# Requesting expert weights and K/V rows in two halves on one DMA queue

## The chip, the cores and the metric

The kernel runs on one core of a Trainium2 chip. The core has five engines that run side by side: TensorE (PE; its weight loads are PEld), VectorE (DVE), ScalarE (ACT), GpSimd (POOL) and SyncE (SP), which here only issues DMA requests. All DMA requests of SyncE go into one queue that 16 DMA engines work off. The metric is the device time of one execution in microseconds; the median of several runs is compared.

## The reference, cut to what matters

Attention with a pooled K/V, and behind it a mixture of experts that sends every row to one expert:

```python
# attention: q (4, 12288, 128), kv (4, 384, 32, 128)
kv_pool = kv.reshape(B, H // 4, 4, W // 4, 4, C).mean(axis=(2, 4))
k = v = kv_pool.reshape(B, -1, C) @ w_sr          # 768 rows of 128 for each b
a = softmax(q @ k.T / sqrt(C)); x = a @ v
# experts: 49152 rows of 128, E = 8 experts, F = 1024
expert_idx = argmax((x / |x|) @ (emb / |emb|).T / tau)
for e in range(E):
    h = np.maximum(x[mask] @ w1[e], 0.0)
    out[mask] = gate_w[mask, None] * (h @ w2[e])
```

## The kernel before

**Attention.** The 49152 rows of q are worked off in 96 steps of 512 (`step_ops`). A step has four score tiles of 128 x 768 (`s_mm`, L810), each evicted by VectorE (`s_leave`, L821) and put through an exponential on ScalarE (L840). Products are made of 16-bit high and low parts: the probabilities are split into `phi` (L861, L865) and `plo` (L875, L880), both are turned by DMA transposes on SyncE into `pthi` and `ptlo` (`p_t`, L904), two score tiles at a time, and `av` (L926) multiplies 12 times with pthi and 6 times with ptlo for each tile. From step 21 on q is turned by DMA as well (`q_turn`, L790).

**K/V.** For b = 1 to 3 the rows of K/V come in eight loads each (`kv_load`, L453): 96 partitions, 4 rows (r) of 2048 bytes, 768 KB. Two buffers `kvt` take turns. Four adds (`kv_adds`, L467) fold a load into `pooled`; the first adds rows 2 and 3 to rows 0 and 1. They run on VectorE for b = 1 and 3 and on GpSimd for b = 2, and stand in those engines' order with everything else.

**Routing.** Each group of four steps is ranked by expert (L1008 to L1151), its rows are scattered to `xs_rows` in HBM (L207), and `select` then picks the next eight tiles of 256 rows, one expert a tile.

**Experts.** Weights are split once at the start into 16-bit parts and stored to `w_prep` in HBM (`w_hi`, `w_lo`, `w_store`). A row of a partition holds first-layer high and low (2 x 1024 elements), second-layer high and low (2 x 1024), and then a scale (8 elements, 4 copies of one 32-bit number): 8208 bytes. For tile t, `load_w` (L1568) copies the 128 rows of its expert, 1026 KB, into one of three buffers `wbuf`; the copy is conditional, and is skipped where that buffer already holds the expert. `load` (L1592, L1593) brings the tile's rows, turned, and their gates. A tile has 8 units of 512: `l1` (L1625) multiplies with the first layer, ScalarE and VectorE evict into `hh` (L1632) and `hl` (L1637), `l2` and `l2_lo` (L1661) multiply with the second layer some units later, into `po`. The scale is needed by VectorE: in `o_gate` (L1672), which multiplies the gates with it while the tile is still running, or, for two tiles of eight (`X["om"]`), in `o_out` (L1684) at its end. There are 184 tiles of 256 rows (`NA`) and up to 23 of 128; requests for tiles under `NA - PER` = 176 are made one by one, the rest in fours.

**Order.** Nothing is reordered on the chip: each engine runs its instructions in the order in which they are written, and a request that waits on SyncE holds those behind it. The order comes from a planner (`Plan`): every operation has an engine, a modelled duration, a key and the operations that it waits for; the planner plays the engines forward and takes, on each, the ready operation with the least key. For a DMA it also models the transfer (`dma`, in us) and holds SyncE back while earlier transfers run:

```python
self.moved = max(self.moved, op.end + 0.65) + op.dma
if eng == "SP":
    turned = op.dur > 0.5
    free[eng] = max(free[eng] + (0.55 if turned else 0.0), self.moved - (0.93 if turned else X["ahead"]))
```

`X["ahead"]` is 2.284. A K/V load has a duration of 0.45 and a transfer of 2.6, a turn of p 0.63 and 1.8, a tile's load 2.5 and 0.65; a copy of weights has 0.5 and a transfer of 3.6 for the first three tiles and 0.08 after them, since most copies are skipped. Keys of l2 lie `X["l2"]` = 3.102 units behind those of l1, a unit being an eighth of 14.892.

Of the kernel before, what the change touches and what calls it, by code (L numbers as in the profile page):

```python
# [11 lines left out]
F16 = mybir.dt.float16  # L12
F32 = mybir.dt.float32
# [4 lines left out]
ALU = mybir.AluOpType  # L18
# [12 lines left out]
ENG = {"A": "ACT", "D": "DVE", "P": "POOL"}  # L31
# [7 lines left out]
KV_ADD = {"D": (1.13, 0.6, 0.33, 0.2), "P": (2.4, 1.25, 0.7, 0.45)}  # L39
# [9 lines left out]
    h=13.707, kv=20.916, kvs=2.272, w0=-14.405, start=23.312, early=21.36, wd=12.952, xw=1.718, qd=21, qs=21.178,  # L49
    ql=9.747, em="---------AA-A-A-A-AA-DM-", et=2.859, ec=-0.864, v0=123.118, sd=1, qu=1.461, q0=-66.525, avd=0.626,  # L50
    m=1.052, end=-3.563, ne=-4.766, ge=-0.689, kd="DPD", gk=547.052, wq="AADADDAD", kv1=10.617, kvs1=0.757, tg=-0.003,
# [8 lines left out]
def attention_moe(  # L60
# [11 lines left out]
    nc = tc.nc  # L72
    V = nc.vector
    P = 128
    B, N, C = q.shape
    H, W = kv.shape[1], kv.shape[2]
    E, _, F = w1.shape
    NT = B * N
    R = 4
    NI, NJ = H // R, W // R  # L80
# [13 lines left out]
    PER = G * Q // T  # L94
    NSEL = NGRP - LAG
    NA = NSEL * PER
# [7 lines left out]
    XB = 6  # L104
    PTB = 4
    PB = 3
    Q2 = 3
    NP = 6
    QB = 2
    NQR = 8  # L110
    WC = 4 * F + 8
    WD = 4 * F + 32
    SCALE = 1.0 / math.sqrt(C)
    PSC = 16384.0
    QSC = 16384.0
# [2 lines left out]
    KF = X["kf"]  # L118

    xs = nc.dram_tensor("xs_rows", (NROW, RP), F32).ap()  # L120
    wprep = nc.dram_tensor("w_prep", (E * P, WD), F16).ap()[:, :WC]
    qf = q.rearrange("b n c -> (b n) c")

    cpool = ctx.enter_context(tc.tile_pool(name="cpool", bufs=1))
# [12 lines left out]
        out=window.rearrange("p (g q) -> p g q", q=4), in_=ident.rearrange("p (g m q) -> p g q m", m=4, q=4), axis=AX.X,  # L137
        op=ALU.add,
# [5 lines left out]
        out=tri16, in_=ones16, pattern=[[1, P]], compare_op=ALU.is_gt, fill=0.0, base=0, channel_multiplier=-1  # L144
# [55 lines left out]
    nt_i = cpool.tile([P, 1], I32, name="nt_i")  # L200
    off_i = cpool.tile([P, NTILE], I32, name="off_i")
    wi_i = cpool.tile([P, NTILE], I32, name="wi_i")
    cpool.tile([P, 72], F32, name="fill")
    ctx.enter_context(tc.manual_schedule())

    def scatter(dst, idx, src, bound, key, skip=()):
# [47 lines left out]
    class Plan:  # L254
# [9 lines left out]
        def add(self, eng, dur, key, fn, *deps, dma=None, take=None, free=None, hold=False, lands=False, port=False):  # L264
            op = Op(eng, dur, key, fn, deps, dma, take, free, hold, lands, port, self.stage)
            self.ops.append(op)
            return op
# [23 lines left out]
        def run(self, begin):  # L291
# [23 lines left out]
            while any(count):  # L315
# [7 lines left out]
                for eng in soon:  # L323
                    if now.setdefault(eng, []):
                        t = free.get(eng, 0.0)
# [77 lines left out]
                            free[eng] + (0.55 if turned else 0.0), self.moved - (0.93 if turned else X["ahead"])  # L403
                        )
                for u in op.users:
                    if op.dma is not None and u.dma is not None and eng == u.eng and not op.lands:
                        ready = op.end
                    elif op.dma is not None:
                        ready = self.moved + X["dma"]
                    else:  # L410
                        ready = op.end + lat.get((eng, u.eng), 0.0)
                    u.ready = max(u.ready, ready)
                    u.left -= 1
                    if not u.left:
                        put(u)
# [33 lines left out]
    def kv_load(b, h):  # L449

        t = kvs.tile([P, WD // 2], F32, tag="kvt", name=f"kvt{b}_{h}", bufs=2)
        t = t[:NI, : R * QC].rearrange("p (r c) -> p r c", r=R)
        nc.sync.dma_start(  # L453
            out=t, in_=kv[b].rearrange("(i r) w c -> i r (w c)", r=R)[:, :, h * QC : (h + 1) * QC]
        )
        st[b]["kvt", h] = t

    def kv_pooled(b, h):
        if h == 0:
# [739 lines left out]

    def w_out(e, i):  # L1200

        wo = xp.tile([P, 2 * F + 8 * i], F16, tag=f"wo{i}", name=f"wo{e}_{i}", bufs=1)
        ws[e]["wo", i] = wo
        if i:
            inv = ws[e]["inv"]
            V.tensor_tensor(
                out=wo[:, 2 * F :].bitcast(F32), in0=inv[:, 0:1].broadcast_to([P, 4]),
                in1=inv[:, 1:2].broadcast_to([P, 4]), op=ALU.mult,
            )

    def w_mul(e, i):
# [6 lines left out]
    def w_hi(e, i):  # L1218
        if i == 0:
            w_out(e, 0)  # L1220
        hi = ws[e]["wo", i][:, 0:F]
        if w_eng(e, i) == " AD":
            nc.scalar.mul(hi, ws[e]["w", i], ws[e]["s"][:, i : i + 1])
        else:
            nc.scalar.copy(out=hi, in_=ws[e]["w", i])

    def w_lo(e, i):
        hi, lo = (ws[e]["wo", i][:, h * F : (h + 1) * F] for h in range(2))
        if w_eng(e, i) == " AD":
            V.scalar_tensor_tensor(  # L1230
                out=lo, in0=ws[e]["w", i], scalar=ws[e]["s"][:, i : i + 1], in1=hi, op0=ALU.mult, op1=ALU.subtract
            )
        else:
            nc.gpsimd.tensor_tensor(out=lo, in0=ws[e]["w", i], in1=hi, op=ALU.subtract)
# [2 lines left out]
        return W_MODES[X["we"][2 * e + i]]  # L1237

    def w_store(e, i):
        nc.sync.dma_start(out=wprep[e * P : (e + 1) * P, 2 * i * F : WC if i else 2 * F], in_=ws[e]["wo", i])  # L1240


    def setup(key, *deps):
# [319 lines left out]
    def load_w(t):  # L1563
        if NA <= t < NA + 2:
            wbuf.append(kvs.tile([P, WD], F16, tag="kvt", name=f"wbuf{WB + t - NA}", bufs=2))
        w = value("w", wi_i, t, E * P + 4096)
        row = nc.s_assert_within(w, 0, (E - 1) * P, skip_runtime_bounds_check_because="the copy is skipped then")
        nc.sync.dma_start(out=wbuf[turn_of(t)][:, :WC], in_=wprep[ds(row, P), :], cond=w < E * P)  # L1568

    xr, late = [], []  # L1570
    ML = 18
# [29 lines left out]
    def turn_of(t):  # L1601
        return t % WB if t < NA else (WB, WB + 1, *[(NA + i) % WB for i in range(WB)])[(t - NA) % (WB + 2)]

    def weights(t, a, n):
        return wbuf[turn_of(t)][:, a : a + n]
# [48 lines left out]
    def l2_terms(t, u, h, parts):  # L1654

        n = size(t)
        fu, nj = 512 // n, n // P
        terms = [(kk, j, o) for kk in range(fu) for j in range(nj) for o in parts]
        for i, (kk, j, o) in enumerate(terms):
            f = 2 * F + (u * fu + kk) * P + o  # L1660
            nc.tensor.matmul(  # L1661
                ts[t]["po"][:, j * C : (j + 1) * C], h[:, kk * n + j * P : kk * n + (j + 1) * P], weights(t, f, P),
                start=u == 0 and i == 0 and len(parts) == 2,
                stop=u == units(t) - 1 and i == len(terms) - 1 and len(parts) == 1, skip_group_check=True,
            )
# [3 lines left out]

    def o_gate(t):  # L1670
        m = ts[t]["m"][:, :, 0:1]
        V.tensor_scalar(out=m, in0=m, scalar1=weights(t, 4 * F, 2).bitcast(F32), scalar2=None, op0=ALU.mult)  # L1672

    def o_out(t):
        m = ts[t]["m"]
        nj = size(t) // P
        if gated(t):
            o = ts[t]["o"] = wk2.tile([P, nj, C], F32, tag="o", name=f"o{t}", bufs=OB)
            po = ts[t].pop("po").rearrange("p (j c) -> p j c", c=C)
            for j in range(nj):  # L1680
                nc.scalar.mul(o[:, j, :], po[:, j, :], m[:, j, 0:1])  # L1681
            return
        o = wk2.tile([P, nj, C], F32, tag="o", name=f"o{t}", bufs=OB)
        V.scalar_tensor_tensor(  # L1684
            out=o, in0=ts[t].pop("po").rearrange("p (j c) -> p j c", c=C),
            scalar=weights(t, 4 * F, 2).bitcast(F32), in1=m[:, :, 0:1].broadcast_to([P, nj, C]),
            op0=ALU.mult, op1=ALU.mult,
        )
        ts[t]["o"] = o
# [19 lines left out]
    def turn(tag, bufs):  # L1709

        u = uses.setdefault(tag, [])
        return (u[-1][:1] if u else []) + (u[-bufs] if len(u) >= bufs else [])

    def took(tag, op):
        uses[tag].append([op])
        return op

    def reads(tag, *ops):
        uses[tag][-1].extend(ops)

    x_wsr = add("ACT", 0.1, -60.0, lambda: nc.scalar.dma_start(out=wsr[:, 0:C], in_=w_sr), dma=0.2)
    x_tau = add("ACT", 0.1, -60.0, lambda: nc.scalar.dma_start(out=tau_b, in_=tau.broadcast_to([P, 1])), dma=0.06)
    x_emb = add("ACT", 0.1, -60.0, lambda: nc.scalar.dma_start(out=emb_sb, in_=emb), dma=0.02)
# [24 lines left out]
    def kv_ops(b):  # L1748
        mine = [None] * NQR
        for h in range(NQR if b else 0):  # L1750
            ahead, apart = (X["kv1"], X["kvs1"]) if b == 1 else (X["kv"], X["kvs"])
            t0 = slot(b * SPB, -8 * (ahead - h * apart))
            o = took("kvt", add("SP", 0.45, t0, lambda h=h: kv_load(b, h), *turn("kvt", 2), dma=2.6, hold=True))
            deps = turn("pooled", 1) if h == 0 else mine[h - 1 : h]
            r = None
            on = X["kd"][b - 1]
            for i, fn in enumerate(kv_adds(b, h, V if on == "D" else nc.gpsimd)):
                r = add(ENG[on], KV_ADD[on][i], t0 + 8.0 + 0.1 * i, fn, o, r, *deps, port=True)
                reads("kvt", r)
            if h == 0:  # L1760
                took("pooled", r)
            mine[h] = r
# [397 lines left out]
    for t in range(NTILE):  # L2160
# [14 lines left out]
            "SP", 0.5 if t < NA - PER else 0.2 if t % 4 else 1.2, kw, lambda t=t: load_w(t), *deps[:2], *stores, *wb_turn(t),  # L2175
            dma=3.6 if t < WB or first or NA + 1 < t < NA + 7 else 0.08, hold=first,
        ))
        o1, o2, ol = None if whole else o1, None, None
        f = 512 / size(t)
        for u in range(nu):  # L2180
            key = s + (u + X["m"]) * w
# [76 lines left out]
```

## Time and profile before

| | us |
|---|---|
| median of 3 runs (lowest, highest) | 1948.01 (1947.91, 1948.92) |
| profiled execution | 1946.91 |
| its span, first to last instruction | 1945.2 |
| busy: TensorE / weight loads | 1906.0 / 1676.3 |
| busy: VectorE / ScalarE / GpSimd | 1675.1 / 1468.7 / 1289.4 |

The span is what the trace covers; 1.7 us of the execution lie around it. An engine's busy time is a union over its instructions. SyncE computes nothing: its rows are requests, each from the moment it is taken up to the moment it is issued, so that a row that is long for its kind waited for something, data or room. Windows give the busy time of each engine in a stretch, the granted TensorE clock (1.00 is 2.4 GHz, 0.50 is 1.2 GHz) and the busy share of the 16 DMA engines, which counts a packet's whole time where it starts and so can pass 1.

### The profile page before, as it was taken

What the parts mean: (1) busy time and instruction counts of PE and PEld (TensorE: products, weight loads), DVE (VectorE), ACT (ScalarE), POOL (GpSimd) and SP (SyncE); (2) the same over time, 40 slices, a digit from 0 to 9 for tenths busy, and PEclk for the clock granted to TensorE, in tenths of its full rate; (3) what the DMA queues carried; (4) which work ended last, traced back from release to release, by engine and by line L of the source; (5) the groups of instructions that cost most, each with busy time, mean ns of one, the idle gap of its engine ahead of it and who ended that gap; (6) DMA issues with size and microseconds to landing.
All of it is one profiled execution on the core that took longest, in us unless ns stands there. A gap on an engine that the chain in (4) does not pass through costs nothing. (4 is left out here: it accounts for less than half of the span.)

```text
span 1945.2 us, 63642 instructions
## 1 busy us (share of the span) xinstructions
PE 1906.0 (98%) x23536; PEld 1676.3 (86%) x23536; DVE 1675.1 (86%) x4037; ACT 1468.7 (76%) x3162; POOL 1289.4 (66%) x1857
## 2 busy tenths in 40 slices
PE   6999999999999999999999999999999999999998
PEld 5787788888888888888888888888888888889998
DVE  7899999988989879989989988998888888886655
ACT  4887877877787778877778877878878788775553
POOL 2547587678777777676676675756756766666654
PEclk9999999999999999999999999999999999999999
DMA  7998989889988999878989899887878677664353
GB/s 258 250 267 207 205 174 183 165 156 164 170 182 173 190 205 175 172 165 157 193 168 175 180 214 180 171 157 155 176 132 173 149 153 152 148 126 86 107 131 109
DMA packets 870922, 333.23 MB, mean 171 GB/s; under 512 B 825794, under 2 KB 836171, under 8 KB 868432
## 3 DMA queue, kind: packets, MB, share of 16 engines
q1 hardware_dynamic: 844624, 274.95, 71.4%
q0 software_dynamic: 24640, 53.53, 9.7%
q8 instruction: 186, 3.05, 0.7%
q14 instruction: 128, 1.05, 0.2%
q10 hardware_dynamic: 1344, 0.66, 0.1%
HBM read 271.41 MB, written 63.19 MB: 172 GB/s over the span
## 5 line engine op out<-in xcount | busy, mean ns | idle before, releaser
L1632 ACT ACTIVATE hh<-ph 128x512 f16<-128x512 f32 x754 | 447.6, 595 | 224.4 <-PE ph L1625 181.2
L1637 DVE SCALAR_TENSOR_TENSOR hl<-ph,hh 128x512 f16<-128x512 f32 x754 | 513.6, 684 | 109.6 <-ACT hh L1632 103.7
L1625 PE MATMUL ph<-x,wbuf 128*128 128x256 f16 x4416 | 593.2, 273 | 3.2 <-DMA wbuf<-w_prep 2.5
L207 POOL DMA_INDIRECT xs_rows<-rows,pi x384 | 442.0, 1151 | 176.5 <-issue 37.8
L207 POOL DMA_INDIRECT out_dram<-o,m x350 | 382.4, 1093 | 229.0 <-ACT o L1681 45.8
L1625 PEld LDWEIGHTS <-wbuf 128*128 128x128 f16 x4848 | 438.9, 98 | 67.4 <-DMA wbuf<-w_prep 2.9
L1661 PE MATMUL po<-wbuf,hh 128*128 128x128 f16 x6032 | 459.9, 219 | 2.9 <-DVE hl L1637 1.1
L1661 PEld LDWEIGHTS <-hh 128*128 128x128 f16 x6176 | 400.0, 98 | 20.6 <-issue 3.8
L810 PE MATMUL s<-k,qT 128*128 128x512 f16 (+1 forms) x1920 | 364.9, 326 | 1.4 <-DVE nm L821 1.4
L821 DVE CUSTOM_DVE_ANT_0 p<-s,scales,qa 128x768 f32<-128x768 f32 x320 | 323.4, 1011 | 41.6 <-PE s L810 38.9
L875 DVE SCALAR_TENSOR_TENSOR plo<-p,phi 128x768 f16<-128x768 f32 x358 | 350.3, 980 | 5.6 <-ACT phi L861 2.4
L840 ACT ACTIVATE p<-p,nm 128x768 f32<-128x768 f32 x320 | 299.0, 934 | 58.8 <-DVE nm L821 56.8
L926 PE MATMUL xp<-v,pthi 128*128 128x136 f16 (+1 forms) x4392 | 319.7, 223 | 1.4 <-ACT q L738 0.8
L1661 PE MATMUL po<-wbuf,hl 128*128 128x128 f16 x3016 | 291.6, 219 | 0.0
L926 PEld LDWEIGHTS <-pthi 128*128 128x128 f16 x4392 | 278.7, 98 | 14.4 <-issue 2.3
L861 ACT ACTIVATE phi<-p 128x768 f16<-128x768 f32 x310 | 260.9, 844 | 5.9 <-DMA pthi<-phi 2.8
L810 PEld LDWEIGHTS <-qT 128*128 128x128 f16 x1920 | 178.6, 98 | 87.4 <-issue 2.3
L1661 PEld LDWEIGHTS <-hl 128*128 128x128 f16 x3088 | 205.1, 98 | 0.6
L926 PE MATMUL xp<-v,ptlo 128*128 128x136 f16 x2196 | 189.8, 223 | 4.3 <-DMA ptlo<-plo 4.3
L946 ACT ACTIVATE x<-xp,rn 128x135 f32<-128x135 f32 x304 | 96.5, 372 | 76.3 <-DVE rn L938 58.2
L960 POOL TENSOR_TENSOR rows<-x,rows 128x256 f16<-128x256 f32 x192 | 137.2, 719 | 18.2 <-ACT rows L956 13.3
L926 PEld LDWEIGHTS <-ptlo 128*128 128x128 f16 x2196 | 144.0, 98 | 4.8 <-DMA ptlo<-plo 4.8
(416 smaller groups left out, 2043.0 us busy)
## 6 DMA issues: line engine op xcount, KB each, us to landing
wbuf<-w_prep SPq DMA_DIRECT2D x202, 1026.0 KB
q<-in_q_dram SPq DMA_DIRECT2D x48, 512.0 KB
kvt<-in_kv_dram SPq DMA_DIRECT2D x24, 768.0 KB
wf<-in_moe_w_dram SPq DMA_DIRECT2D x16, 512.0 KB
kvt<-in_kv_dram SPq DMA_DIRECT2D x12, 512.0 KB
xs_rows<-rows,pi POOLq DMA_INDIRECT x384
out_dram<-o,m POOLq DMA_INDIRECT x350
w_prep<-wo SPq DMA_DIRECT2D x8, 514.0 KB
```

The lines of the kernel that those rows point to most:

```text
L207: ins = nc.gpsimd.indirect_dma_start(out=dst, out_offset=bass.IndirectOffsetOnAxis(ap=idx, axis=0), in_=src, in_offset=None, bounds_check= ...
L810: nc.tensor.matmul(t[:, lo:hi], qs[:, l, :], r[:, lo:hi], start=i == 0, stop=i == 2)
L821: V.tensor_tensor_reduce(out=p, in0=ks[k].pop(("s", j)), in1=scales[:, 4:5].broadcast_to([P, NK]), scale=ks[k]["fac"], scalar=3.0e38, op0= ...
L840: nc.scalar.activation(out=p, in_=s, func=AF.Exp, bias=ks[k].pop(("nm", j)), scale=1.0 if unscaled(k) else -1.0)
L861: nc.scalar.mul(hi, p, PSC)
L875: V.scalar_tensor_tensor(out=lo, in0=ks[k].pop(("p", j)), scalar=PSC, in1=hi, op0=ALU.mult, op1=ALU.subtract)
L926: nc.tensor.matmul(ks[k]["xp", h][:, i, :e], l[:, c, :], r[:, c, :e], start=n == 0, stop=n == len(terms) - 1, skip_group_check=True,)
L960: nc.gpsimd.tensor_tensor(out=r[:, :, C : 2 * C], in0=ks[k]["x"][:, 2 * h : 2 * h + 2, 0:C], in1=r[:, :, 0:C], op=ALU.subtract)
L1625: nc.tensor.matmul(ph[:, kk * n : (kk + 1) * n], weights(t, o + f, P), r, start=i == 0, stop=i == 2)
L1632: nc.scalar.activation(out=hh, in_=ts[t]["ph", u], func=AF.Relu)
L1637: V.scalar_tensor_tensor(out=hl, in0=ts[t].pop(("ph", u)), scalar=0.0, in1=ts[t]["hh", u], op0=ALU.max, op1=ALU.subtract)
L1661: nc.tensor.matmul(ts[t]["po"][:, j * C : (j + 1) * C], h[:, kk * n + j * P : kk * n + (j + 1) * P], weights(t, f, P), start=u == 0 and i ...
```

## The change

A row of `w_prep` becomes 8256 bytes: the scale moves from the end to the place between the two layers and is 32 elements wide. For tiles under 176 the copy is requested in two halves, first layer and scale, then second layer; the second half has the same condition. l1 and the scaling of the gates read the first half, l2 the second. Loads of K/V are requested in two halves of two rows (r) each; the first add waits for both. `second` makes the request of the second half: an operation of no duration on SyncE whose key is lower than all others, behind an operation on an engine `"~t"` that stands for nothing on the chip and takes 1.5 us (`HALF`) from the modelled end of the first request. Whole copies remain for tiles from 176 on.

```diff
+    HALF = 1.5
-    WC = 4 * F + 8
-    WD = 4 * F + 32
+    WS = 32
+    WD = 4 * F + WS
...
-                    if op.dma is not None and u.dma is not None and eng == u.eng and not op.lands:
+                    if op.dma is not None and u.dma is not None and eng == u.eng and not op.lands or u.eng == "~t":
                         ready = op.end
...
     def kv_load(b, h):
...
+        kv_part(b, h, 0)
+
+    def kv_part(b, h, i):
+        r = slice(i * (R // 2), (i + 1) * (R // 2))
         nc.sync.dma_start(
-            out=t, in_=kv[b].rearrange("(i r) w c -> i r (w c)", r=R)[:, :, h * QC : (h + 1) * QC]
-        )
+            out=st[b]["kvt", h][:, r, :],
+            in_=kv[b].rearrange("(i r) w c -> i r (w c)", r=R)[:, r, h * QC : (h + 1) * QC],
+        )
...
-                out=wo[:, 2 * F :].bitcast(F32), in0=inv[:, 0:1].broadcast_to([P, 4]),
-                in1=inv[:, 1:2].broadcast_to([P, 4]), op=ALU.mult,
+                out=wo[:, 0:WS].bitcast(F32), in0=inv[:, 0:1].broadcast_to([P, WS // 2]),
+                in1=inv[:, 1:2].broadcast_to([P, WS // 2]), op=ALU.mult,
...
-        nc.sync.dma_start(out=wbuf[turn_of(t)][:, :WC], in_=wprep[ds(row, P), :], cond=w < E * P)
+        if t >= NA - PER:
+            nc.sync.dma_start(out=wbuf[turn_of(t)], in_=wprep[ds(row, P), :], cond=w < E * P)
+            return
+        ts[t]["w"] = w, row
+        w_part(t, 0)
+
+    def w_part(t, i):
+        w, row = ts[t]["w"]
+        c = slice(2 * F + WS, WD) if i else slice(0, 2 * F + WS)
+        nc.sync.dma_start(out=wbuf[turn_of(t)][:, c], in_=wprep[ds(row, P), c], cond=w < E * P)
...
+    def second(o, key, fn):
+
+        return add("SP", 0.0, -1e6, fn, add("~t", HALF, key, lambda: None, o))
...
             o = took("kvt", add("SP", 0.45, t0, lambda h=h: kv_load(b, h), *turn("kvt", 2), dma=2.6, hold=True))
+            rest = second(o, t0, lambda h=h: kv_part(b, h, 1))
...
-                r = add(ENG[on], KV_ADD[on][i], t0 + 8.0 + 0.1 * i, fn, o, r, *deps, port=True)
+                r = add(ENG[on], KV_ADD[on][i], t0 + 8.0 + 0.1 * i, fn, o, r, rest, *deps, port=True)
...
-        o1, o2, ol = None if whole else o1, None, None
+        lw2 = second(lw, kw, lambda t=t: w_part(t, 1)) if t < NA - PER else lw
+        o1, o2, ol = None if whole else o1, lw2, None
```

The other edits follow the new layout: the places of the split parts in `w_hi`, `w_lo` and `w_store`, the places that `l2_terms`, `o_gate` and `o_out` read, and 256 bytes less of an unused tile.

## Rows read from the trace of the kernel before

**Rows 1.** The page, busy time of each engine (share of the span), xinstructions.
```profile
PE 1906.0 (98%) x23536; PEld 1676.3 (86%) x23536; DVE 1675.1 (86%) x4037; ACT 1468.7 (76%) x3162; POOL 1289.4 (66%) x1857
```

**Rows 2.** Windows: stretch, length, busy us (x) PE, PEld, DVE, ACT, POOL; clock, DMA, GB/s.
```profile
0.00:50.00 50.00, 35.02 (x129) 25.25 (x130) 38.37 (x111) 23.13 (x33) 11.09 (x32) 0.97 0.79 262
...
700.00:750.00 50.00, 46.57 (x596) 41.09 (x595) 40.27 (x90) 35.38 (x79) 35.62 (x46) 1.00 0.98 188
...
1900.00:1950.00 50.00, 39.44 (x687) 38.26 (x684) 23.34 (x43) 16.72 (x28) 18.65 (x20) 0.96 0.26 79
```

**Rows 3.** Waits: engine, line, waited for: us in total, times, longest us.
```profile
PE xp L926 <- DMA ptlo<-plo: 4.3, 2, 2.3
...
PE ph L1625 <- DMA wbuf<-w_prep: 2.5, 2, 2.1
...
PE rk L1100 <- DVE oh L1086: 0.9, 1, 0.9
...
DVE m L1672 <- DMA wbuf<-w_prep: 3.9, 3, 2.5
```

**Rows 4.** Timeline of PE: start, us, instruction, form, xcount [idle before <-releaser].
```profile
535.35 0.53 PE L926 MATMUL xp<-v,ptlo 128*128 128x136 f16 x6 [2.00 <-DMA ptlo<-plo]
...
705.56 0.88 PE L926 MATMUL xp<-v,pthi 128*128 128x136 f16 x12 [0.41 <-DMA pthi<-phi]
708.74 0.53 PE L926 MATMUL xp<-v,ptlo 128*128 128x136 f16 x6 [2.29 <-DMA ptlo<-plo]
...
1163.98 0.83 PE L1625 MATMUL ph<-x,wbuf 128*128 128x256 f16 x6 [2.13 <-DMA wbuf<-w_prep]
```

**Rows 5.** Windows of PE alone after the wait at 1162: busy (x), clock, DMA, GB/s.
```profile
1165.00:1168.00 3.00, 3.00 (x18) 0.50 1.07 191
1168.00:1169.00 1.00, 1.00 (x12) 0.78 0.45 76
```

**Rows 6.** Timeline of SyncE, first and last of nine copies that move, tiles under 176.
```profile
216.92 0.38 SPq L1568 DMA_DIRECT2D wbuf<-w_prep  x1
...
1157.61 0.35 SPq L1568 DMA_DIRECT2D wbuf<-w_prep  x1
```

**Rows 7.** Timeline of SyncE, 521 to 533.
```profile
521.84 0.64 SPq L453 DMA_DIRECT2D kvt<-in_kv_dram  x1
522.58 1.44 SPq L904 DMA_TRANSPOSE pthi<-phi  x1
...
526.17 2.29 SPq L790 DMA_TRANSPOSE qT<-q  x1
528.50 3.88 SPq L904 DMA_TRANSPOSE ptlo<-plo  x1
```

**Rows 8.** Timeline of SyncE, 691 to 706.
```profile
691.24 0.36 SPq L1568 DMA_DIRECT2D wbuf<-w_prep  x1
...
694.53 0.64 SPq L453 DMA_DIRECT2D kvt<-in_kv_dram  x1
...
698.48 5.26 SPq L790 DMA_TRANSPOSE qT<-q  x1
...
704.91 1.42 SPq L904 DMA_TRANSPOSE ptlo<-plo  x1
```

**Rows 9.** Windows, the hole: busy of all engines, clock, DMA share, GB/s.
```profile
529.00:530.00 1.00, 1.00 (x22) 1.00 (x20) 1.00 (x4) 0.94 (x2) 0.66 (x2) 1.00 0.04 5
```

**Rows 10.** Instructions of L1568: duration ns min/median/max, first and last start us; forms.
```profile
L1568 SPq FUSED_REGOPS  x202: 174/202/207, 216.6 to 1927.2; - x101
...
L1568 SPq DMA_DIRECT2D wbuf<-w_prep x202: 73/88/384, 216.9 to 1928.8; - x101
```

**Rows 11.** Adds of L467: idle time of their engines before them (us, times), ended by.
```profile
  DMA kvt<-in_kv_dram: 7.2, 5
```

**Rows 12.** Timelines of GpSimd and VectorE at 747.
```profile
747.17 2.36 POOL L467 TENSOR_TENSOR kvt<-kvt 96x1024 f32<-96x1024 f32 x1 [2.80 <-DMA kvt<-in_kv_dram]
...
747.54 2.14 DVE L1075 TENSOR_TENSOR d<-x,mx 128x128 f32<-128x128 f32 x1
```

More of the change, by code (lines that the diff above doesn't have):

```diff
@@ L120, in attention_moe @@
     xs = nc.dram_tensor("xs_rows", (NROW, RP), F32).ap()
-    wprep = nc.dram_tensor("w_prep", (E * P, WD), F16).ap()[:, :WC]
+    wprep = nc.dram_tensor("w_prep", (E * P, WD), F16).ap()
     qf = q.rearrange("b n c -> (b n) c")
@@ L202, in attention_moe @@
     wi_i = cpool.tile([P, NTILE], I32, name="wi_i")
-    cpool.tile([P, 72], F32, name="fill")
+    cpool.tile([P, 8], F32, name="fill")
     ctx.enter_context(tc.manual_schedule())
@@ L451, in kv_load @@
         t = kvs.tile([P, WD // 2], F32, tag="kvt", name=f"kvt{b}_{h}", bufs=2)
-        t = t[:NI, : R * QC].rearrange("p (r c) -> p r c", r=R)
+        st[b]["kvt", h] = t[:NI, : R * QC].rearrange("p (r c) -> p r c", r=R)
+        kv_part(b, h, 0)
+    def kv_part(b, h, i):
+        r = slice(i * (R // 2), (i + 1) * (R // 2))
         nc.sync.dma_start(
-            out=t, in_=kv[b].rearrange("(i r) w c -> i r (w c)", r=R)[:, :, h * QC : (h + 1) * QC]
+            out=st[b]["kvt", h][:, r, :],
+            in_=kv[b].rearrange("(i r) w c -> i r (w c)", r=R)[:, r, h * QC : (h + 1) * QC],
         )
-        st[b]["kvt", h] = t
     def kv_pooled(b, h):
@@ L1200, in w_out @@
     def w_out(e, i):
-        wo = xp.tile([P, 2 * F + 8 * i], F16, tag=f"wo{i}", name=f"wo{e}_{i}", bufs=1)
+        wo = xp.tile([P, 2 * F + WS * i], F16, tag=f"wo{i}", name=f"wo{e}_{i}", bufs=1)
         ws[e]["wo", i] = wo
@@ L1220, in w_hi @@
             w_out(e, 0)
-        hi = ws[e]["wo", i][:, 0:F]
+        hi = ws[e]["wo", i][:, WS * i : WS * i + F]
         if w_eng(e, i) == " AD":
@@ L1227, in w_lo @@
     def w_lo(e, i):
-        hi, lo = (ws[e]["wo", i][:, h * F : (h + 1) * F] for h in range(2))
+        hi, lo = (ws[e]["wo", i][:, WS * i + h * F : WS * i + (h + 1) * F] for h in range(2))
         if w_eng(e, i) == " AD":
@@ L1239, in w_store @@
     def w_store(e, i):
-        nc.sync.dma_start(out=wprep[e * P : (e + 1) * P, 2 * i * F : WC if i else 2 * F], in_=ws[e]["wo", i])
+        nc.sync.dma_start(out=wprep[e * P : (e + 1) * P, 2 * i * F : WD if i else 2 * F], in_=ws[e]["wo", i])
     def setup(key, *deps):
@@ L1659, in l2_terms @@
         for i, (kk, j, o) in enumerate(terms):
-            f = 2 * F + (u * fu + kk) * P + o
+            f = 2 * F + WS + (u * fu + kk) * P + o
             nc.tensor.matmul(
@@ L1671, in o_gate @@
         m = ts[t]["m"][:, :, 0:1]
-        V.tensor_scalar(out=m, in0=m, scalar1=weights(t, 4 * F, 2).bitcast(F32), scalar2=None, op0=ALU.mult)
+        V.tensor_scalar(out=m, in0=m, scalar1=weights(t, 2 * F, 2).bitcast(F32), scalar2=None, op0=ALU.mult)
     def o_out(t):
@@ L1685, in o_out @@
             out=o, in0=ts[t].pop("po").rearrange("p (j c) -> p j c", c=C),
-            scalar=weights(t, 4 * F, 2).bitcast(F32), in1=m[:, :, 0:1].broadcast_to([P, nj, C]),
+            scalar=weights(t, 2 * F, 2).bitcast(F32), in1=m[:, :, 0:1].broadcast_to([P, nj, C]),
             op0=ALU.mult, op1=ALU.mult,
```

## The prediction

> **What bounds the kernel now.** I read the page first. TensorE is busy 1906.0 us of a span of 1945.2; the other engines stand at 86% or less [rows 1]. Only less idle time of TensorE, 39 us in all, or a higher clock on it can shorten the run. The windows say where those 39 us lie: 15 in the first 50 us and 6 in the last 45, which the change hardly touches; of the rest the stretch from 700 to 750 has most, 3.4 us [rows 2]. TensorE's waits, grouped, name what the change can reach: two waits for ptlo, 4.3 us, and two for an expert copy, 2.5 us [rows 3]. The timeline puts them in place: 2.00 us at 533.35 for ptlo; 0.41 for pthi and 2.29 for ptlo between 705 and 709; 2.13 us at 1161.85 for wbuf [rows 4]. The last costs more than its own length. The granted clock stood at 1.00 (2.4 GHz) while TensorE waited and is 0.50 (1.2 GHz) from 1165 to 1168, 0.78 in the microsecond after [rows 5]. At half speed 3 us lose 1.5, and 0.22 more: 1.7 us.
>
> SyncE's timeline then shows what stood in the queue. At 1162 it was the copy itself, requested at 1157.61 [rows 6]. At 533 and 706 a K/V load was requested 6.7 and 10.4 us before ptlo, at 706 with an expert copy 3.3 us ahead of that; behind them requests of a kind that takes 1.4 us when it runs freely hold SyncE 2.3 to 5.3 [rows 7, 8]. A window of one microsecond in the first place shows a hole: from 529 to 530 the DMA engines are busy 0.04, with ptlo already being issued [rows 9]. So these two waits are partly volume and partly holes.
>
> **The change part by part.** The order that the planner writes stays: a second half takes no time on its SyncE and adds no modelled transfer; it becomes ready 1.5 us after the first request's modelled end and then goes first. After a K/V load the model holds SyncE 0.97 us, and a turn of 0.63 follows, so one request (pthi at 522.58, say) falls between the halves. After a copy of a tile past the third (modelled transfer 0.08) the next request follows at once and the second half comes behind it. For tiles 0 to 2 (modelled at 3.6) SyncE is held 1.97 us, more than 1.5, and nothing falls between.
>
> *Expert copies.* 176 requests are halved, but a request that moves data takes 0.34 to 0.38 us on SyncE and a skipped one some 0.09; nine of these 176 move, the first at 216.92, the last at 1157.61 [rows 6, 10]. At 1162 the first half is what l1 needs. l1 started 6.4 us after the request. If all of that were data, the first half would be there after 3.2 us, at 1160.8; if 2 us of it were fixed, after 4.2, at 1161.8. TensorE comes free at 1161.85: the wait of 2.13 goes, and the slow clock behind it, 1.7. The second half stands behind one turn and is asked for near 1159.7; at the whole copy's 6.4 us it would land by 1166. The tile's first use of it is l2 of its first unit, 3.1 units of 1.86 us behind l1 by the planner's keys, past 1167. Term: -3.8. Bounds: 0 if l2 waits instead, -3.8.
>
> *Skipped second halves.* 167 of them, each 202 ns for the address and 88 for the request [rows 10], 0.29 us, 48 us beside other work. They cost nothing while transposes land before TensorE wants them, and of all pairs of pthi and ptlo TensorE noticed only those in [rows 3, 4]. Where that cover is gone, at 533 and 706, it is 0.29 more per place. Taken: 0.
>
> *K/V loads.* 24 loads become 48 requests, 0.64 us more on SyncE each [rows 7]. The half moves pthi ahead by half a load, some 2 us. ptlo, however, is the fourth request behind the load in both places, so both halves still go before it: by volume it lands when it did, and nothing is saved. By the holes it may: SyncE's 2.29 and 3.88 us for qT and ptlo at 526 to 532 fall to 1.4 each if the queue in front is shorter, which is 3.4 us in the place where 2.00 are lost. Bounds: +3.6 (0.64 + 0.29 at both places, and one slow clock of 1.7, since 2.00 would then exceed the 2.13 that brought one) to -4.7 (2.00 + 2.70). I take half of the best, -2.3: the hole is as near a row as the volume is.
>
> Against this speaks a rule of the Trainium skill (DMA: Bandwidth & Descriptors, section Anatomy of one DMA): every transfer carries about 2 us that don't shrink with its size, so two halves are dearer than one whole. The rows show that part overlapped: pthi, qT and ptlo are requested 2 to 4 us apart behind the load and the queue keeps moving. By the page's figure, an estimate, 33 more moving transfers would add 66 us of transfer time; as a mechanism it is the fourth rival.
>
> *Adds on K/V.* The first add of a load needs both halves, so it starts later by the request put between: 1.44 us where that runs freely, 5.26 where it is held [rows 7, 8]; I take 2.4, nearer the free one. The adds stand in order on VectorE (16 loads) or GpSimd (8), with everything behind them. Five began the moment the load landed, after waits of 7.2 us in all [rows 11]; these wait 2.4 longer each, 12 us. What reaches TensorE is small: GpSimd's wait of 2.80 at 744 to 747 pushed its add onto VectorE's d, 2.14 us beside it, and TensorE lost 0.9 on the one-hot that follows d [rows 3, 12]; 0.9 of 7.2 us of waits is 13%. Term: +1.5. Bounds: 0 to +7.5 (all 24 late by 2.4, at 13%).
>
> *Gate before the copy has landed whole.* VectorE waited 3.9 us for copies in three gate scalings [rows 3]; part of that goes, and since TensorE's list has no wait on such a scaling I count it as 0. *The scale's place*: 16 instead of 4 elements in eight small multiplies, stores of 520 instead of 514 KB, late whole copies 6 KB longer: under 0.1 us, 0.
>
> **Sum.** -3.8 - 2.3 + 1.5 = -4.6. The profiled execution took 1946.91 (its span and 1.7 around it), so 1942.3; the median shown is 1.1 above it: 1943.4.
>
> **Rivals.** *Only the copy's wait goes.* ptlo lands as before: -3.8 + 1.5, 1945.7. For it: the volume ahead of ptlo is unchanged. Against: the hole. *All three waits go*: -3.8 - 4.7 with adds harmless, 1939.5. For it: 3.4 us of SyncE's blocked time at 533. Against: at 706 the copy, the load and three transposes really fill the queue. *Slower: late adds.* The second half waits on SyncE behind a transpose that waits for its data; such requests hold SyncE up to 5.26 us [rows 8]. Then VectorE stands still in front of the adds, with scores' and hl's evictions behind, and TensorE's two score banks fill. At 13% all 24 cost 7.5, the K/V waits stay and lengthen by 1.9: -3.8 + 7.5 + 1.9 = +5.6, 1953.6. It decides from an added wait of about 4 us at the five adds without slack. Against: VectorE idles 14% of the span. *Each half pays its own fixed part*: the copy's wait only halves and its slow clock goes (-2.8), the K/V waits lengthen (+1.9), the adds cost their 1.5: 1948.6, within the bound. Against: the overlap above. *The wait moves to l2*: 0 - 2.3 + 1.5, 1947.2, within. Against: the margin of more than 1 us at 1166. That nothing falls between the halves leaves the copy's term, since l1 waits on the first half all the same.
>
> **Chances.** Forecast 38% (its own range 1941 to 1946); all three go 20%; only the copy 20%; slower 13%; fixed part 4%; l2 5%. A measurement of this kernel can tell about 0.2%, 3.9 us, from no change, so faster means under 1944.1: two thirds of the forecast, the whole of the second, a quarter of the third, 0.50; slower 0.13; same 0.37. The range reaches from below the case of all three to the middle between no change and the slower case: 1938 to 1950.
>
> **What would show it.** Right: no wait on wbuf in TensorE's list before 1800 and no clock of 0.50 at 1165; at 533 and 706 waits of ptlo under 1.2 us; waits on kvt on GpSimd and VectorE up from 7.2 to some 19 us. Wrong: TensorE waiting in l2 (L1661's line) on wbuf; new waits of scores on VectorE; ptlo waits above 2 us with a clock of 0.50 behind them.

## The result, and the profile after

The changed kernel took 1968.3 us (median of six runs, 1963.9 to 1971.9) against 1947.95 (1942.1 to 1948.9) for the kernel before in the same series: 20 us slower by the medians, and a ratio of 1.0115 [1.0099, 1.0131]. Forecast were 1943.4, a range to 1950, and 13% for slower. The order of the instructions on TensorE, VectorE, ScalarE and GpSimd is the same in both traces; only SyncE's list differs, by the second halves.

The page and the windows of the changed kernel (span 1969.9; the lines named here are 5 to 14 higher: L453 is L458, L467 is L472, L1568 is L1582, L1625 is L1639). First the busy line, to be read against [rows 1]:

```profile
PE 1912.3 (97%) x23536; PEld 1680.5 (85%) x23536; DVE 1678.3 (85%) x4037; ACT 1469.9 (75%) x3162; POOL 1292.6 (66%) x1857
```

Then windows of TensorE alone: stretch, length, busy (x), clock, DMA share, GB/s.

```profile
50.00:1220.00 1170.00, 1136.23 (x13574) 0.99 0.88 182
1220.00:1500.00 280.00, 276.96 (x3520) 1.00 0.78 160
1500.00:1850.00 350.00, 349.94 (x4570) 1.00 0.66 135
```

The same windows of the kernel before:

```profile
50.00:1220.00 1170.00, 1153.05 (x13877) 1.00 0.92 186
1220.00:1500.00 280.00, 278.87 (x3538) 1.00 0.81 162
1500.00:1850.00 350.00, 349.59 (x4582) 1.00 0.63 132
```

Of 24.7 us of span, 16.8 are idle time of TensorE before 1220. Busy time grew by 6.3, although the work is the same: behind three stops the granted clock is lower, 0.57, 0.50 and 0.58 over the four microseconds from 454, 770 and 963; the kernel before has one such place up to 1900 [rows 5]. From 1500 on nothing is lost, though the skipped second halves go on to 1860. Matched instruction by instruction, TensorE's delay is 25.0 us at 1215 us of the kernel before (its tile 103), and still 25.0 at 1800.

What TensorE waited for, and who else waited for SyncE's transfers (waits: engine, line, waited for: us in total, times, longest), to be read against [rows 3, 11]:

```profile
...
PE ph L1639 <- DVE hl L1651: 10.4, 4, 5.6
...
PE ph L1639 <- DMA wbuf<-w_prep: 3.5, 2, 1.8
PE ph L1639 <- DVE qa L729: 2.9, 1, 2.9
PE rk L1116 <- DVE cn L1109: 2.8, 3, 1.9
PE xp L931 <- DMA ptlo<-plo: 2.4, 1, 2.4
PE po L1675 <- ACT o L1695: 2.1, 2, 1.2
PE ph L1639 <- DVE kvt L472: 1.8, 1, 1.8
...
POOL kvt L472 <- DMA kvt<-in_kv_dram: 18.2, 4, 8.3
...
DVE kvt L472 <- DMA kvt<-in_kv_dram: 6.0, 3, 3.4
```

The waits named by the forecast shrank little in sum, from 6.8 to 5.9 us: ptlo from 4.3 to 2.4, while wbuf grew from 2.5 to 3.5. New or much longer are waits on work of VectorE and ScalarE (hl, qa, cn, o, kvt), the longest 5.6 us. The largest can be followed back through four engines. SyncE's timeline of the changed kernel (start, us to issue, request):

```profile
746.33 2.95 SPq L795 DMA_TRANSPOSE qT<-q  x1
749.37 0.53 SPq L458 DMA_DIRECT2D kvt<-in_kv_dram  x1
750.91 0.07 SPq L1582 DMA_DIRECT2D wbuf<-w_prep  x1
751.72 1.22 SPq L1606 DMA_TRANSPOSE x<-xs_rows  x1
753.21 0.39 SPq L1607 DMA_DIRECT2D m<-xs_rows  x1
753.64 0.47 SPq L458 DMA_DIRECT2D kvt<-in_kv_dram  x1
754.52 0.08 SPq L1582 DMA_DIRECT2D wbuf<-w_prep  x1
```

and GpSimd, VectorE and TensorE behind it:

```profile
758.98 2.35 POOL L472 TENSOR_TENSOR kvt<-kvt 96x1024 f32<-96x1024 f32 x1 [8.31 <-DMA kvt<-in_kv_dram]
...
768.46 0.25 POOL L1329 TENSOR_SCALAR t_nt_i<-t_cnt 128x8 int32<-128x8 f32 x1
...
768.74 0.68 DVE L1332 TENSOR_SCALAR t_nt_j<-t_nt_i 128x8 int32<-128x8 int32 x1 [6.13 <-POOL t_nt_i L1329]
...
770.61 1.44 PE L1639 MATMUL ph<-x,wbuf 128*128 128x256 f16 x6 [5.57 <-DVE hl L1651]
```

The first half of the load goes out at 749.37, the second 4.3 us later, behind a skipped copy half, a tile's rows and its gates. GpSimd stands 8.31 us before the add; the routing behind it on GpSimd is late; VectorE stands 6.13 us for that; TensorE's next eviction lies behind it on VectorE, 5.57 us. At 962 it is the load of q: ScalarE stood 4.54 us for it until 960.65, and TensorE 2.88. A single trace doesn't fix these places, though. In a second trace of the changed kernel (`j3_after`, below) the stop near 770 is there again (TensorE's delay grows by 4.8 us between 750 and 800 of the kernel before, 6.5 here), but the delay at 1215 is 13.2 us, not 25.0.

At the expert copies the first half didn't win either (SyncE, then TensorE):

```profile
1169.89 0.34 SPq L1582 DMA_DIRECT2D wbuf<-w_prep  x1
1170.98 1.21 SPq L1606 DMA_TRANSPOSE x<-xs_rows  x1
1172.46 0.40 SPq L1607 DMA_DIRECT2D m<-xs_rows  x1
1173.27 0.33 SPq L1582 DMA_DIRECT2D wbuf<-w_prep  x1
...
1181.95 0.34 SPq L1582 DMA_DIRECT2D wbuf<-w_prep  x1
```

```profile
1175.28 0.83 PE L1639 MATMUL ph<-x,wbuf 128*128 128x256 f16 x6 [1.61 <-DMA wbuf<-w_prep]
...
1186.68 0.83 PE L1639 MATMUL ph<-x,wbuf 128*128 128x256 f16 x6 [1.85 <-DMA wbuf<-w_prep]
```

The last moved copy was requested 4.24 us before TensorE came free in the kernel before (1161.85 - 1157.61, [rows 4, 6]), and 2.88 before it now (1184.83 - 1181.95). What the shorter transfer gains, the later request has lost. Only the slow clock is gone: behind both waits the granted clock stayed at 1.00 (1176 to 1180, 1187 to 1191).

Last, what a request of a half costs SyncE (duration ns min/median/max):

```profile
L1582 SPq FUSED_REGOPS  x352: 187/200/212, 217.1 to 1859.8; - x176
L1582 SPq MOVE wbuf<-w_prep x352: 29/29/38, 217.4 to 1860.1; - x176
L1582 SPq DMA_DIRECT2D wbuf<-w_prep x352: 73/81/389, 217.4 to 1860.1; - x176
L1582 SPq EVENT_SEMAPHORE  x226: 17/17/28, 217.3 to 1860.0; - x113
```

Four short instructions, with gaps between them: from the end of what is before to the start of what is behind, a median of 0.53 us over the 352 halves. The forecast had 0.29.

### The profile page after: what moved, and what is told of

Same layout as the page of the kernel before. It is cut to its first block, busy times and chain, and to the rows that moved or that the text cites. A ratio compares the mean times of both kernels' runs of the same rounds, so it can differ in the third digit from the quotient of the medians.

```text
span 1969.9 us, 64360 instructions
## 1 busy us (share of the span) xinstructions
PE 1912.3 (97%) x23536; PEld 1680.5 (85%) x23536; DVE 1678.3 (85%) x4037; ACT 1469.9 (75%) x3162; POOL 1292.6 (66%) x1857
## 5 line engine op out<-in xcount | busy, mean ns | idle before, releaser
L1639 PE MATMUL ph<-x,wbuf 128*128 128x256 f16 x4416 | 594.3, 273 | 19.5 <-DVE hl L1651 10.4
L208 POOL DMA_INDIRECT xs_rows<-rows,pi x384 | 444.2, 1157 | 178.6 <-issue 39.4
L1639 PEld LDWEIGHTS <-wbuf 128*128 128x128 f16 x4848 | 439.1, 98 | 84.5 <-issue 17.6
```

The costliest lines, as they stand in the source:

```text
L208: ins = nc.gpsimd.indirect_dma_start(out=dst, out_offset=bass.IndirectOffsetOnAxis(ap=idx, axis=0), in_=src, in_offset=None, bounds_check= ...
L1639: nc.tensor.matmul(ph[:, kk * n : (kk + 1) * n], weights(t, o + f, P), r, start=i == 0, stop=i == 2)
```

## The experiments

Theory A: the adds on K/V are late because other requests lie between the halves. Theory B: SyncE is full in the first 1220 us; each skipped half costs it 0.53 us, and whatever stands behind is that much later. Rivals C and D are in the texts on record. Times are medians, ratios against the kernel before in the same series.

**Which part.** Four kernels: the copies' halves and the new layout alone; the K/V halves alone; the layout alone; the whole change with the two K/V requests next to each other.

```diff
 e1_copies_only:  kv_load, kv_adds as before
 e2_kv_only:      layout, load_w and lw as before
 e3_layout_only:  WS = 32 and its offsets alone; load_w one request as before
 e4_kv_together:  the change, and
-  rest = second(o, t0, lambda h=h: kv_part(b, h, 1))
+  rest = second(o, t0, lambda h=h: kv_part(b, h, 1), 0.0)   # "~t" takes 0.0, not HALF
```

> The expert copies stay in halves, with the scale between the layers; loads of K/V are whole again. Theory A (the adds on K/V start too late): the loss of some 20 us goes, 1943 to 1950, with no wait of GpSimd on kvt above 3 us. Theory B (the 167 skipped second halves make SyncE late for everything): the loss stays, 1960 or more. Theory C (new layout of the weights in HBM and in the buffer): stays too.

> Only the loads of K/V are in halves; copies of weights are whole, their layout as before. Theory A: most of the loss is here, 1962 to 1970, with waits on kvt of 6 to 8 us on GpSimd near 440 and 755. Theory B: under 1953. Theory C: 1948.

> The scale lies between the layers and rows of 8256 bytes are copied, every copy and every load whole. Theories A and B: 1948, within 3 us. Theory C: 1955 or more.

> Everything in halves as in the changed kernel, but the second half of a K/V load is requested straight behind the first. Theory A, in the form that the request put between is what makes the add late: 1945 to 1951. Theory A, in the form that any second request of K/V costs: above 1957. Theory B: 1960 or more.

| kernel | us | ratio |
|---|---|---|
| copies only | 1962.1 | 1.0090 [1.0065, 1.0115] |
| K/V only | 1951.5 | 1.0035 [1.0023, 1.0048] |
| layout only | 1944.7 | 1.0000 [0.9987, 1.0012] |
| change, K/V halves together | 1960.6 | 1.0082 [1.0057, 1.0106] |

The layout costs nothing. The separated K/V halves cost 7 us, and only when separated: put together, the whole change stands where the copies alone stand. The larger part, some 17 us, is the copies. With them alone ScalarE waits 25.0 us for q, against 18.2 before; in the changed kernel, which is slower, it is 19.3, so this one sum doesn't follow the cost.

**What about the copies.** Four kernels more: one request that is never taken, besides whole copies; halves requested one straight behind the other; halves only from tile 108 on, where all copies are skipped; halves only for the nine tiles whose copy moves with this data.

```diff
 f1_never_taken (kernel before; `fill` is a scrap, placed by second() behind the copy):
+  nc.sync.dma_start(out=fill.bitcast(F16)[:, :16], in_=wprep[ds(row, P), :16], cond=w < 0)
 f2_halves_together (copies only):
   w_part(t, 0)
+  w_part(t, 1)
-  lw2 = second(lw, kw, lambda t=t: w_part(t, 1)) if t < NA - PER else lw
 f3_halved_from_108, f4_halved_where_moved (copies only; whole copies elsewhere):
+  def halved(t):
+    return 108 <= t < NA - PER                         # f3
+    return t in (0, 1, 2, 48, 49, 50, 96, 97, 98)      # f4
-  if t >= NA - PER:
+  if not halved(t):
-  lw2 = second(lw, kw, lambda t=t: w_part(t, 1)) if t < NA - PER else lw
+  lw2 = second(lw, kw, lambda t=t: w_part(t, 1)) if halved(t) else lw
```

> The kernel before, its copies whole, with one more conditional request of SyncE for each whole tile at the place where the change puts the second half; its condition is never true and its target is a scrap of SBUF that nothing reads, so it waits for nothing and moves nothing. Theory B (SyncE is full in the first 1220 us, each request that it skips costs it some 0.5 us, and the loads of q, K/V and the transposes behind it come that much later): most of what the halved copies alone cost, 1955 to 1962 us, with ACT's wait for q above its 18.2 us and PE's delay constant from about 1220 us on. Rival C (the copies' halves cost by their own waits and by their transfers lying between other requests): 1943 to 1947, as the kernel before.

> The halved copies alone, the second half requested straight behind the first. Theory B (the number of requests decides): 1956 to 1963, as with other requests between the halves (1962.1). Rival C (the place of the second half, its wait and what it comes ahead of, decides): 1944 to 1950.

> Halved copies for the whole tiles from number 108 on alone (none of these copies is taken, so there are only skipped second halves, some 68 of them); the tiles before have whole copies. Theory B: nothing, 1943 to 1946, since from 1220 us on SyncE has room and no transpose or load of K/V is left to be late. Rival D (a skipped request costs the same wherever it is): 68 of 167 of some 17 us, so 7 us more, 1950 to 1952.

> Halved copies only for the nine whole tiles whose copy is taken with this data (numbers 0 to 2, 48 to 50, 96 to 98); all other copies are one request as before, so there are 9 requests more and not 176. Theory B: the cost is gone, 1942 to 1946, and what is left is what halving does to the moved copies themselves. Rival C (the moved halves lie between other requests and delay them): still 1955 to 1962.

| kernel | us | ratio |
|---|---|---|
| one never-taken request a tile | 1949.3 | 1.0029 [1.0017, 1.0040] |
| copy halves together | 1972.2 | 1.0140 [1.0109, 1.0171] |
| halved from tile 108 on | 1944.3 | 1.0002 [0.9993, 1.0012] |
| halved where moved | 1945.4 | 1.0009 [0.9999, 1.0019] |

A request that moves nothing and waits for no other work costs time, so rival C, by which only the halves' own transfers and waits cost, does not suffice. It costs nothing from tile 108 on, whose copy is requested at 1255 us in the kernel before: rival D falls. The reason given on record, that no transpose is left to be late there, is wrong: transposes of p go on there, in the kernel before until 1755 us. With the 167 skipped halves gone, and the nine moved ones kept, the cost is gone, and so is the hoped-for gain: the wait at the copy is 2.75 us, no shorter than before [rows 4].

```profile
1167.26 1.07 PE L1638 MATMUL ph<-x,wbuf 128*128 128x256 f16 x6 [2.75 <-DMA wbuf<-w_prep]
```

Two expectations missed. The never-taken request cost 5.7 us, between the ranges of theory B and rival C and less than the halves; it is also cheaper on SyncE, 0.35 us, because it works out no new address:

```profile
L1573 SPq MOVE  x176: 29/29/38, 217.9 to 1841.6; - x176
L1573 SPq MOVE fill<-w_prep x176: 29/29/52, 218.0 to 1841.7; - x176
L1573 SPq DMA_DIRECT2D fill<-w_prep x176: 54/79/109, 218.0 to 1841.8; - x176
```

And the halves together cost 27 us, with 0.50 us each on SyncE, against 17 apart. The intervals, 21 to 33 and 13 to 22 us, just overlap, so that the place counts beside the time is likely here, not shown; why it should be the worse place stays open.

**Dose, and SyncE relieved.** Two never-taken requests a tile; the K/V halves together with whole copies; and, the other way round, SyncE given time back. For every tile it loads two registers (the tile's row in `xs_rows`, the expert's row in `w_prep`), one by one up to tile 175 and in fours after that. Dropping the first case loads all in fours.

```diff
 g1_two_never_taken:  the never-taken request twice
 g3_kv_together_only: K/V only, the second half straight behind the first
 g2_values_by_four (kernel before), g4_copies_by_four (copies only):
     def value(name, src, t, top):
-        if t < NA - PER:
-            return nc.sync.value_load(src[0:1, t : t + 1], min_val=0, max_val=top)
         i = t // 4 * 4
```

> The kernel before with two never-taken requests for each whole tile in place of one: 0.70 us of SyncE a tile (two of the 0.35 us that one measured), a third more than the 0.53 us of a skipped half. One of 0.35 us cost 5.7 us of time. Theory B (SyncE's time alone, with a reserve that is used up first): 1957 to 1970, at or above the halved copies alone (1962.1). Rival C (what the halves cost beyond 6 us lies in their transfers and waits): twice one request's cost at most, 1952 to 1956.

> The kernel before with the two register loads of a tile (its row in xs_rows and its row in w_prep) done for four tiles at a time, as the last tiles have it already: some 0.5 us or more of SyncE less for three tiles of four on each load. Theory B backwards (SyncE's lateness already costs the kernel before something): faster, 1937 to 1942, with ACT's wait for q and PE's wait for ptlo smaller. Rival (the kernel before has just enough room on SyncE): 1943 to 1945, the same.

> K/V loads alone in two halves, the second requested straight behind the first, copies whole. Theory A (the requests between the halves cost, since the adds wait for the second half): 1943 to 1946, as the kernel before, against 1951.5 with requests between. Rival (two requests in place of one cost by themselves): 1949 to 1953.

> The halved copies alone (1962.1 as measured, 17 us above before), with the register loads done for four tiles at a time as in the run with the kernel before. Theory B: the halves' 0.53 us of SyncE a tile is given back by the loads, and most of the cost goes: 1942 to 1950. Rival C (the halves cost by transfers and waits, not by SyncE's time): 1957 to 1963.

| kernel | us | ratio |
|---|---|---|
| two never-taken requests a tile | 1955.7 | 1.0067 [1.0043, 1.0090] |
| K/V halves together, whole copies | 1944.7 | 1.0001 [0.9990, 1.0013] |
| before, registers by four | 1935.4 | 0.9960 [0.9941, 0.9979] |
| copies halved, registers by four | 1936.6 | 0.9956 [0.9943, 0.9969] |

Two never-taken requests cost 13 us, which lies in rival C's range (1952 to 1956) and just under theory B's (1957 to 1970). They measured 0.55 us of SyncE together, though, not the 0.70 that B's range was worked out from: 0.35 us a tile for 5.7 us and 0.55 for 13, and the separated halves with 0.53 us (17, interval 13 to 22) can't be told from that. This run decides nothing between B and C. The halved copies with registers by four do: by C the halves should still cost some 17 us there, and they cost 1.3. The loads show how much was given back. Kernel before, then the kernel before by four:

```profile
L1554 SPq FUSED_REGOPS  x352: 147/164/187, 216.2 to 1831.9; - x176
...
L1554 SPq TENSOR_LOAD <-wi_i x176: 263/542/1214, 215.2 to 1831.6; - x176
L1554 SPq TENSOR_LOAD <-off_i x176: 263/288/957, 217.4 to 1813.2; - x176
```

```profile
L1555 SPq TENSOR_LOAD <-wi_i x51: 298/323/1450, 215.8 to 1915.2; - x51
...
L1555 SPq TENSOR_LOAD <-off_i x51: 296/347/777, 217.6 to 1910.4; - x51
```

One load of four registers takes about as long as a load of one, and the operations behind each load go. With gaps, from 200 to 1220, it is 1.70 us of SyncE a tile before and 0.33 after. (The Trainium skill, DMA: Bandwidth & Descriptors, section Latency and other measured facts, puts the floor of a register load at some 0.6 us and says that unrolling by four amortizes it. The second agrees; the floor here is 0.26 us.) The kernel before was thus itself short of SyncE's time, by some 8 us, and the halved copies cost 1.3 us more than whole ones, nothing that can be told apart.

**Is K/V's cost the same thing?** The first two runs fell on a chip on which the kernel before took 2015.6 us, so they were made again in one series with their ground and with the change itself.

```diff
 h1_after_by_four, j2_after_by_four: the changed kernel, registers by four
 h2_kv_by_four:                      K/V only, registers by four
 j1_before_by_four:                  the kernel before, registers by four
 j3_after:                           the changed kernel
```

> The changed kernel as it is, with the register loads done for four tiles at a time. Theory B alone (all of the 20 us lost is SyncE's fullness): 1934 to 1939, as the kernel before with loads by four (1935.4). Theory A beside B (the separated K/V halves keep their own cost of some 7 us, the adds waiting for a second half behind other requests): 1940 to 1945.

> The K/V loads alone in two separated halves (1951.5 as measured, 7 us above before), copies whole, with the register loads by four. If the lateness of the second half comes from SyncE's fullness: 1934 to 1938. If the requests between the halves cost by themselves: 1940 to 1944.

> The kernel before with the register loads by four, as the ground for the next two on the same chip: 0.996 of the kernel before, as measured.

> The changed kernel with the register loads by four. Theory B alone: the same as the kernel before by four, 0.996 of before within 0.0015. Theory A beside B (the separated K/V halves keep a cost of their own): 3 to 7 us above it, 0.9975 to 1.0.

> The changed kernel itself on the same chip: 1.010 to 1.013 of before, as measured; what the loads by four give back of it is the distance to the run above.

| kernel | us | before, same series | ratio |
|---|---|---|---|
| change, by four (other chip) | 2006.8 | 2015.6 | 0.9961 [0.9943, 0.9978] |
| K/V only, by four (other chip) | 2005.7 | 2015.6 | 0.9943 [0.9920, 0.9966] |
| before, by four | 1937.4 | 1945.1 | 0.9962 [0.9949, 0.9975] |
| change, by four | 1938.0 | 1945.1 | 0.9958 [0.9944, 0.9971] |
| change | 1964.0 | 1945.1 | 1.0098 [1.0066, 1.0129] |

The whole change, K/V halves apart as they were, costs nothing once SyncE has room; the loads by four are worth 8 us to the kernel before and 26 us to the changed one. Theory A's mechanism is real, as 749 to 770 shows, but it is theory B's shortage that makes it cost. The waits of the changed kernel by four:

```profile
POOL kvt L472 <- DMA kvt<-in_kv_dram: 6.2, 3, 3.7
...
ACT qjunk L715 <- DMA q<-in_q_dram: 5.2, 4, 3.9
...
PE ph L1637 <- DVE hl L1649: 2.4, 4, 1.5
...
DVE kvt L472 <- DMA kvt<-in_kv_dram: 1.1, 1, 1.1
...
PE xp L931 <- DMA ptlo<-plo: 0.3, 1, 0.3
```

GpSimd's and VectorE's waits for K/V are 7.3 us, not 24.2; TensorE has no wait on wbuf at all, and 0.3 on ptlo. The kernel before by four has 1.3 and 0.5 there, so what the halves remove with room is about 1.5 us, too little to be seen in the time. The fastest kernels of this study are those with registers by four, and with or without halves they are equal.

**How full is SyncE?** Theory B's word is too strong. Summed over its waits for other engines and for landings from 200 to 1220 us, SyncE stood idle for 354 us in the kernel before and 307 in the changed one, 479 and 425 in the same two with registers by four. So it is not short of time as a whole; what it lacks is time in certain stretches. Nor is there more room later: in the kernel before it stood idle for 242 of 630 us from 1220 to 1850. Yet in every trace here but the two from the slower chip TensorE's delay, or gain, is made before 1215 us of the kernel before; from 1255 to 1800 none moves by more than 1 us. Transposes of p (21 in 100 us), loads of q and skipped halves go on there as before. What ends are the K/V loads (last request at 1192) and the copies that move (1157). That SyncE's time costs only beside those is likely, but no run left them out, so it is not shown.

## Why the prediction was wrong

*Skipped second halves: the step that failed.* "167 of them, each 202 ns for the address and 88 for the request, 0.29 us, 48 us beside other work. They cost nothing while transposes land before TensorE wants them." The number was right. The duration was nearly half too small (0.53 with what stands around it, 88 us), and the cover was the wrong one. The argument looked at pairs of pthi and ptlo and found slack. The skipped half also delays loads of q, K/V loads, and the requests of the copies themselves, and these end as waits of ScalarE, GpSimd and VectorE, with TensorE's evictions behind them. Measured: 17 us for the copies alone, and with SyncE relieved 1.3, which can't be told from 0. The list of TensorE's waits couldn't show it: it names the engine that TensorE waits for last, and in the kernel before only some 7 us there (ptlo, wbuf, pthi) point to SyncE's transfers, while ScalarE alone waits 18.2 us for q.

*Expert copies, -3.8.* Failed: +1.8 [-0.2, 3.7] where the moved copies alone are halved. The landing was estimated well: whole copies took 6.0 us from request to landing (mean of nine), first halves 4.1 (mean of the nine in that run), against the 4.2 of the case with 2 us fixed. Twice 4.1 less 6.0 gives 2.2 us that don't shrink, an estimate. The Trainium skill (DMA: Bandwidth & Descriptors, section Anatomy of one DMA) gives about 2 us, for transfers that GpSimd issues, not for every transfer as the prediction has it; for SyncE's copies this run agrees. What failed is the request's time, taken as unchanged. In that run it went out at 1163.04, TensorE came free 1.5 us later, at 1164.51, and the half landed at 1167.21; in the kernel before TensorE came free 4.24 us after the request.

*K/V loads, -2.3, and adds, +1.5.* Together -0.8, measured +7. The wait at 533 went and the one at 706 stayed, but that proves nothing for the halves: with nine halved copies and whole K/V loads ptlo's waits are 2.4 us in one place as well. Where the prediction has one request between the halves of a load, 0 to 3 fell between them in the changed kernel; that put the halves 2.1 us apart on average, near the 2.4 taken, and up to 5.3. The added waits, 7.2 us that were to become some 19, became 24.2, but that they came near is partly luck: K/V halves alone made it 13.0, the copies' halves alone 11.4. Their price was wrong: 13% of an added wait, taken from one place. It was TensorE's share where VectorE's work was slowed, not where GpSimd stood still with the routing behind it. The rival of late adds had the mechanism: the second half behind other requests, and the added wait of 4 us from which it decides. Its price for the K/V part, 7.5 and 1.9, lies above the 7 measured. It was given 13%, and its cause, that SyncE itself is short of time where this happens, was not seen.

*The scale's place: 0*, measured 0. *The wait moves to l2*, and *each half pays its own fixed part* as the whole story: TensorE's list has no wait on wbuf in l2, and K/V halves requested together cost nothing.

## What to carry to other kernels

A queue engine with no arithmetic has a budget like any other: count a request with its address arithmetic, register loads and gaps before it is called free, even one that is skipped. A sum over the whole run is not enough, since here SyncE stood idle a third of the time and still came late. What tells is a dose: add a request that is never taken, or take bookkeeping away, and see whether the time moves. Look for the cover of a later request in the waits of every engine behind it, not only of the one that sets the end. Where a queue engine is short, cheaper bookkeeping (registers in fours) was worth more here than any finer cut of the transfers.

## What the runs showed of the hardware

A conditional request that is not taken occupies SyncE for 0.53 us when it works out its own address and 0.28 to 0.35 when it doesn't. A transposition's request can hold SyncE long after its data is there, when a moving copy and a K/V load lie ahead of it: with nine halved copies a pthi taken at 1140.78 was issued at 1147.17, although ScalarE had written its phi by 1142.53; the copy's second half landed at 1146.56 and the load at 1145.37. In the kernel before the one at that place was issued at 1143.04, its phi written by 1139.86, the load landed at 1142.46. A free one takes 1.4 us. That it waits for the transfers ahead is how the times lie; no run took them away. And one chip ran the same programs 3.6% longer (2015.6 us), with TensorE busy 1927.9 us in the changed kernel by four, against 1903.4 on another chip, and with 48 stops of up to 1.5 us before l1, l2 and av, 24.6 us together, for which the trace names no engine or transfer; why is open. The ratio of the loads by four was the same there, 0.996.
